# Two Fourier and gated layers on one core: separate homes for the last block's row tiles, a later difference step, a gap in the tests, and a new order of the opening

## The chip, the cores and the metric

The kernel runs on one core of a Trainium2 chip. The metric is device time in microseconds (us), the median of several runs. One more execution was taken with the hardware profiler; all views of the profile come from it.

## The reference

The input `x` is 2048 rows by 640 columns. Two layers follow each other, each of them a Fourier mixing step and a gated step, both with a residual:

```python
def _A_ref(x, dft_seq_re, dft_seq_im, dft_hid_re, dft_hid_im):
    a = jnp.einsum("bsd,ed->bse", x, dft_hid_re)
    b = jnp.einsum("bsd,ed->bse", x, dft_hid_im)
    return jnp.einsum("ts,bse->bte", dft_seq_re, a) - jnp.einsum("ts,bse->bte", dft_seq_im, b)

def _B_ref(x, w_gate, w_up, w_down):
    g = jnp.einsum("bsd,df->bsf", x, w_gate)
    u = jnp.einsum("bsd,df->bsf", x, w_up)
    return jnp.einsum("bsf,fd->bsd", _sigmoid(g) * u, w_down)

x = A_x
for _ in range(2):
    x = x + _A_ref(_layernorm(x), ...)
    x = x + _B_ref(_layernorm(x), ...)     # w_gate, w_up: 640 x 1728, w_down: 1728 x 640
```

## The kernel before

All matrix work is done in 16-bit floats, each operand as a high half and a low half, with three products for one. The Fourier matrices are used through their symmetries: rows and columns are folded onto each other, which cuts the products; the kernel tests on the way that the given matrices have these symmetries, and a general program stands behind it for the case that they haven't. Rows are taken in four blocks of 512 (`block`, `last` is the fourth). In the gated step of most blocks seven products of half size do the work of eight (`seven`, line 1516, by way of `products`, lines 1434 to 1448).

**The opening** (line 1780) is everything until layer 1's first gated products. SyncE's queue issues the loads in a fixed order: the rows of `x` in groups A to D for each of four parts, the Fourier matrices, the hidden ones, the first weights. Then a long table of names, `OPENING` (line 160), is read from left to right; each name calls one function, which emits its instructions. On every engine the instructions stand in that order, and an engine takes them strictly in turn. The names that matter here: `turn i g` lets TensorE reverse the rows of a group with a reversing matrix (line 404), `turned` copies the result back on ScalarE (line 410), `ident 0` makes the second reversing matrix (lines 357 and 358), `stats` takes a group's mean and variance (line 482), `cg` and `col` fold columns (lines 734 and 735), `row n` folds the one odd row, `chi` and `clo` make high and low halves of the Fourier matrix, `join` adds folded rows (line 869), `jhi` and `jlo` make their halves (lines 886 and 896), `seq` is the product along the sequence (line 1035), `ev` and `evhi` take its sums out of PSUM (lines 269 and 271), `nst`, `cen`, `nhi`, `nlo`, `tp`, `tph` and `tpl` are the norm ahead of the gated step: statistics, centring (line 518), high and low halves (lines 544 and 547), transposes on TensorE (line 669) and the copies that follow them (lines 677 and 679). `wshi` and `wslo` split a weight tile. `junk n` emits n small products whose result nobody reads (line 380); they fill TensorE's time while it has nothing else.

**After the opening** the work is a list of steps, one for each piece of TensorE's work. `at(u, f, ...)` puts a function before step `u`; what shares a step is sorted by the fraction of `u`, and `run` puts a list of functions in order at one place. In layer 2 the norm of the first rows stands at `he + 10`: `norm_turned(r, 0)` and `norm_turned(r, 1)` make the halves of row tile `r`, and `first_differences` (line 1192) makes two differences for a sum that is needed later (line 1197).

**Row tiles of a block.** While a block's products run, the next block's rows are prepared in two pairs of row tiles, `i` = 0 and 1. For each, `pair_apply` (line 603) writes the normed rows to a tile `pf`, `pair_combine` (lines 610 to 613) adds combinations, `pair_parts` (lines 621 and 622) writes the halves to a tile `pb`, and `pair_transpose` (line 626) issues two transposing transfers on SyncE's queue from `pb` to the operand that TensorE reads, and gives `pb` back.

**Homes.** Tiles share one large buffer. `take` asks for a number of units and `drop` gives them back; the kernel is first recorded without addresses, `find_homes` (line 99) then places all tiles so that two which are held at the same time do not overlap, the largest first, keeping tiles apart in time where it can, and the kernel is recorded again with these addresses. So a tile that is held longer can change the address of many others, and an instruction that writes to an address waits for the last reader of what was there before. The loads of the products' weights (`G`, `S` and `U` with the tile's number: lines 1362, 1364, 1366 and 1368, in SyncE's queue) are among these. `hv` is a tile of gate values, read last by line 1513.

**Tests.** The tests of the Fourier matrix load rows or columns by GpSimd's queue (lines 1663 and 1680) into a `room`, compare on VectorE (lines 1669 to 1689) and add up squares on ScalarE (line 1635). In layer 1, 42 of them are spread evenly from `block[1] + 6` to `block[3] + 13`: the load at `u`, the test 1.2 and the squares 1.95 spacings later. Two rooms are fixed; a third and further ones are taken from the large buffer when the two are in use.

Of the kernel before, what the change touches and what calls it, by code (L numbers as in the profile page):

```python
# [18 lines left out]
D = 640  # L19
# [119 lines left out]
class Slot:  # L139
# [18 lines left out]


OPENING = """  # L160
    turn 0 B, turned 0 B, stats 0 D, cg 0 3, stats 0 A, cg 0 1, ident 0, turn 0 C, junk 13, turned 0 C, means 0,
    turn 1 C, turn 1 B, chi 0 0, square 0 B, chi 1 0, double 0, square 0 C, turned 1 B, clo 1 0, turned 1 C, junk 13,
    ident 2, stats 1 A, cg 0 2, means 1, square 1 B, power 0, chi 1 1, col 1 0, junk 13, junk 8, scale 0, clo 0 0,
    stats 1 D, cg 0 0, col 1 1, turn 2 B, dg 0, square 1 C, mj 0, turned 2 B, power 1, stats 2 A, turn 2 C,
    turned 2 C, double 1, ps 0, junk 15, double 2, scale 1, junk 10, ro 1 1, chi 1 2, means 2, col 2 1, row 0,
    col 2 0, row 1, clo 1 1, junk 3, turn 3 B, whhi 1, re 1 0, ro 1 0, square 2 B, square 2 C, re 1 1, clo 1 2,
    chi 0 1, whlo 1, stats 2 D, whhi 2, jhi 0 o, junk 14, junk 5, de 1 0, de 1 1, do 1 1, do 1 0, join 1, junk 1,
    whhi 5, chi 0 2, jhi 1 o, power 2, junk 4, whhi 0, scale 2, row 2, turned 3 B, ro 2 0, re 2 0, jhi 0 e, jhi 1 e,
    re 2 1, whlo 5, jlo 0 o, whlo 0, jlo 1 o, clo 0 1, jlo 0 e, turn 3 C, junk 4, junk 5, turned 3 C, free, col 3 0,
    stats 3 A, junk 2, seq 0 1, whhi 3, ro 2 1, c512hi, jlo 1 e, row 3, dd 2 0, seq 1 1, stats 3 D, means 3, col 3 1,  # L170
    c512lo, seq 0 0, evhi 0 1 0, wshi 0 1, evhi 0 1 1, whlo 3, dd 2 1, chi 1 3, square 3 C, square 3 B, ev 0 1 0,
    junk 5, join 2, ev 0 1 1, clo 1 3, power 3, double 3, jhi 2 e, evhi 0 1 2, scale 3, chi 0 3, ro 3 1, seq 1 0,
    re 3 1, junk 14, jhi 2 o, re 3 0, junk 12, whhi 4, ro 3 0, evhi 0 0 0, clo 0 2, jlo 2 e, clo 0 3, ev 0 1 2,
    dd 3 1, junk 18, jlo 2 o, junk 14, dd 3 0, join 3, ident 1, whlo 4, ev 0 0 0, evhi 0 0 2, seq 2 1, jhi 3 e,
    jhi 3 o, wshi 2 0, evhi 0 0 1, wshi 1 1, jlo 3 e, jlo 3 o, seq 2 0, whlo 2, ev 0 0 1, wslo 1 1, ev 0 0 2, seq 3 0,
    seq 3 1, evhi 1 0 1, wshi 2 1, evhi 1 0 0, evhi 1 1 1, hid 0 0, evhi 1 0 2, ev 1 0 0, ev 1 0 1, ev 1 1 1,
    evhi 1 1 2, evhi 1 1 0, wslo 0 1, ev 1 0 2, first 1, first 0, wshi 1 0, hid 0 1, ev 1 1 0, wslo 1 0, im, sums,
    hid 1 0, hidev 1 0, hid 1 1, hid 2 0, add 0, nst 0, hidev 1 1, wshi 0 0, cen 0, difs, add 1, hidev 2 0, nst 1,
    nvar 0, ev 1 1 2, wslo 0 0, npow 0, nscale 0, nst 2, cen 1, nst 3, nhi 0, nhi 1, nvar 1, nlo 0, wld 4 0, wld 4 1,
    cen 3, mid, hid 2 1, nlo 1, npow 1, tp 0, tp 1, tph 0, wld 3 1, wld 3 0, tpl 0, tpl 1, nscale 1, tph 1, cen 2,  # L180
    wslo 2 0, nhi 3, nhi 2, midhi, gu 0 0, hidev 2 1, nlo 2, nlo 3, tp 2, tp 3, tpl 2, tph 3, hid 3 0, wshi 3 0,
    hidev 3 0, hid 3 1, tph 2, wshi 4 1, wshi 3 1, tpl 3, wshi 4 0, hidev 3 1, wslo 3 1, wslo 3 0, gu 1 0, gu 0 1,
    gu 1 1, wslo 2 1, wslo 4 1, middif, wslo 4 0, gu 2 0, gu 2 1"""

ON_ACT = {(2, GA), (2, GD), (3, GA), (3, GD)}
# [41 lines left out]
def folded(ctx, tc, pool, dram, big, acc, flag, homes, x, ct, wh, wg, wu, wc, wd, out):  # L227
# [19 lines left out]
    turn = [0]  # L247
# [46 lines left out]
    def at(u, f, *a):  # L294
        jobs[max(0, int(u // 1))].append((u, f, a))
# [158 lines left out]
    stats = {}  # L454
# [119 lines left out]
    def place(b):  # L574
        return (b + len(other)) % 2
# [47 lines left out]
        if n == 3:  # L623
            drop("pf", b, i)

    def pair_transpose(b, i):
        for q, src in enumerate(held["pb", b, i].parts):
            nc.sync.dma_start(XW[place(b)][:, :, q, i * P : (i + 1) * P], src, transpose=True)  # L628
        drop("pb", b, i)


    FT = XO["T1"]
# [1216 lines left out]
    last = NB - 1  # L1849
# [3 lines left out]
    for layer in range(2):  # L1853
        first = layer == 0
# [9 lines left out]
        block = []  # L1864
# [16 lines left out]
        def run(u, todo):  # L1881
            for n, (f, *a) in enumerate(todo):
                at(u + 0.001 * n, f, *a)

        def evictions(ph, tps=(EV, OD)):
            return [(evict_sums, ph, tp, d) for tp in tps for d in (1, 0, 2)]
# [40 lines left out]
        else:  # L1927
# [3 lines left out]
            odd = [[(f, *key, (n,)) for n in range(2)] for ph in range(2) for f, *key in evictions(ph, (OD,))]  # L1931
# [281 lines left out]
```

## Time and profile before

| | |
|---|---|
| time, median of 3 runs | 1136.33 us (1135.86 to 1137.09) |
| time of the profiled execution | 1136.34 us |
| its span, first to last instruction | 1134.5 us |
| granted TensorE clock | 0.999 |
| busy: PE, PEld, DVE, ACT, POOL | 1118.4, 892.3, 757.5, 539.5, 347.7 us |
| matmuls | 9123 |

PE is TensorE's products, PEld its loads of weights, DVE VectorE, ACT ScalarE, POOL GpSimd, SP SyncE; SPq is SyncE's queue. In the timeline a row gives start, duration, engine, line, operation, tiles and shapes, the count of merged instructions, and in brackets the engine's idle time before it with what ended it. In the view of waits a row gives who waited for whom, the total, the number of times and the longest. Busy time of TensorE counts products that overlap, so the distance from one start to the next tells more than the duration of one.

### The profile page before, as it was taken

The numbers are of one execution on the slowest core, as the hardware profiler recorded it, in microseconds if no ns is written. First come the engines' busy times: TensorE is split into PE (matmuls) and PEld (weight loads), VectorE is DVE, ScalarE is ACT, GpSimd is POOL, SyncE is SP. The second block draws the span as 40 slices with busy tenths as digits, with TensorE's granted clock in tenths as the row PEclk, the third lists the DMA queues.
The fourth block names the chain that finished last, engine by engine and source line by source line (L and its number), as shares of the span: only waits on it lengthen the run. The fifth ranks groups of instructions, "written<-read, shape, count | busy, mean of one in ns | idle before, by whom it ended". The sixth has DMA issues, their size and how long they took to land. (4 is left out here: it accounts for less than half of the span.)

```text
span 1134.5 us, 23654 instructions
## 1 busy us (share of the span) xinstructions
PE 1118.4 (99%) x9123; PEld 892.3 (79%) x9123; DVE 757.5 (67%) x1679; ACT 539.5 (48%) x1191; POOL 347.7 (31%) x568
## 2 busy tenths in 40 slices
PE   7999999999999999999999999999999999999998
PEld 5777446788878887888878888778877888778875
DVE  7984897866656776576668877834764578426751
ACT  7985583355524653265525545214642555225430
POOL 1001653332555452521440203032554222132001
PEclk9999999999999999999999999999999999999999
DMA  8533885777495767968522672575857973799511
GB/s 248 188 106 110 300 319 150 232 232 248 140 264 187 246 183 167 257 221 292 179 99 76 160 228 83 141 235 183 249 174 184 291 232 108 88 237 292 161 42 39
DMA packets 154448, 214.74 MB, mean 189 GB/s; under 512 B 74655, under 2 KB 99505, under 8 KB 154326
## 3 DMA queue, kind: packets, MB, share of 16 engines
q1 hardware_dynamic: 135622, 165.04, 49.5%
q0 software_dynamic: 18560, 47.93, 13.9%
q8 instruction: 73, 1.20, 0.4%
q14 instruction: 49, 0.40, 0.1%
q10 hardware_dynamic: 144, 0.16, 0.0%
HBM read 173.04 MB, written 25.44 MB: 175 GB/s over the span
## 5 line engine op out<-in xcount | busy, mean ns | idle before, releaser
L1445 PE MATMUL acc<-big 128*128 128x256 f16 x4698 | 516.5, 273 | 1.1 <-DMA big<-big 1.1
L1445 PEld LDWEIGHTS <-big 128*128 128x128 f16 x4698 | 459.7, 98 | 55.4 <-issue 1.3
L1602 PE MATMUL acc<-big 128*128 128x320 f16 x2624 | 357.7, 299 | 0.0
L1602 PEld LDWEIGHTS <-big 128*128 128x128 f16 x2624 | 256.8, 98 | 99.5
L1663 POOL DMA_DIRECT2D big<-in_ct x256 | 174.7, 688 | 263.6 <-DVE big L1672 136.0
L1449 ACT ACTIVATE big<-acc 128x256 f32<-128x256 f32 x348 | 130.8, 382 | 242.4 <-PE acc L1445 235.7
L1513 DVE TENSOR_TENSOR big<-big 128x512 f16<-128x512 f32 x87 | 60.0, 689 | 114.1 <-ACT big L1512 114.0
L1635 ACT ACTIVATE big<-big 128x768 f32<-128x768 f32 (+10 forms) x110 | 81.3, 739 | 82.4 <-DVE big L1672 64.2
L1398 PE MATMUL acc<-big 128*128 128x256 f16 (+1 forms) x705 | 114.6, 325 | 0.5 <-ACT big L677 0.5
L1398 PEld LDWEIGHTS <-big 128*128 128x128 f16 x705 | 68.9, 98 | 45.0 <-issue 0.7
L1491 ACT ACTIVATE big<-big 128x512 f32<-128x512 f32 x87 | 53.4, 627 | 50.2 <-DVE big L1482 49.6
L271 DVE SCALAR_TENSOR_TENSOR big<-big 128x640 f16<-128x640 f32 (+7 forms) x82 | 61.2, 778 | 11.8 <-ACT big L269 9.4
L1501 DVE SCALAR_TENSOR_TENSOR big<-acc,big 128x256 f32<-128x256 f32 x87 | 36.4, 419 | 41.4 <-PE acc L1445 35.9
L1617 DVE SCALAR_TENSOR_TENSOR big<-acc,big 128x320 f32<-128x320 f32 x64 | 28.3, 484 | 52.8 <-PE acc L1602 52.7
L621 ACT ACTIVATE big<-big 128x384 f16<-128x384 f32 (+2 forms) x48 | 28.6, 645 | 70.1 <-DVE big L603 48.6
L269 ACT ACTIVATE big<-big 128x640 f16<-128x640 f32 (+7 forms) x82 | 51.3, 657 | 20.8 <-POOL big L1336 6.6
L1482 DVE TENSOR_TENSOR big<-big,acc 128x512 f32<-128x512 f32 x87 | 59.2, 681 | 1.3 <-PE acc L1445 1.1
L1512 ACT ACTIVATE big<-big 128x512 f16<-128x512 f32 x87 | 54.4, 626 | 8.1 <-DVE big L1503 7.0
L1680 POOL DMA_DIRECT2D big<-in_ct x40 | 27.4, 689 | 92.3 <-ACT big L1635 58.3
L442 POOL DMA_INDIRECT out<-big,rows x8 | 9.3, 1165 | 123.3 <-DVE fin L1760 55.1
L1481 DVE TENSOR_TENSOR big<-big 128x256 f32<-128x256 f32 x87 | 36.4, 418 | 7.7 <-ACT big L1449 7.6
L1669 DVE TENSOR_TENSOR big<-big 128x256 f32<-128x256 f32 x64 | 26.5, 415 | 21.5 <-DMA big<-in_ct 21.5
(252 smaller groups left out, 1100.4 us busy)
## 6 DMA issues: line engine op xcount, KB each, us to landing
big<-kept_s SPq DMA_DIRECT2D x84, 512.0 KB, 6.8
big<-kept_w SPq DMA_DIRECT2D x115, 320.0 KB, 5.0
big<-in_ct POOLq DMA_DIRECT2D x256, 128.0 KB, 4.8
big<-kept_w SPq DMA_DIRECT2D x74, 192.0 KB, 5.8
kept_w<-big SPq DMA_DIRECT2D x27, 320.0 KB, 3.4
big<-in_ct POOLq DMA_DIRECT2D x32, 256.0 KB, 5.3
kept_s<-big SPq DMA_DIRECT2D x13, 512.0 KB, 7.1
big<-in_wg SPq DMA_DIRECT2D x18, 320.0 KB, 4.9
```

Source lines behind the costliest of these rows:

```text
L269: nc.scalar.activation(dh, src, AF.Copy, scale=s)
L271: nc.vector.scalar_tensor_tensor(dl, src, s, dh, op0=OP.mult, op1=OP.subtract)
L1398: nc.tensor.matmul(ps, w[wp][:, d * P : (d + 1) * P], xt[:, xp, :], start=(d == 0 and wp == HI and xp == HI), stop=(d == ND - 1 and wp == LO))
L1445: nc.tensor.matmul(ps, wt, xt, start=start and n == 0, stop=n == len(todo) - 1, skip_group_check=not start)
L1449: nc.scalar.activation(dst, ps, AF.Copy)
L1482: nc.vector.tensor_tensor(v, v, other, op=OP.add)
L1491: nc.scalar.activation(v, v, AF.Sigmoid, scale=SG)
L1512: nc.scalar.activation(s.parts[HI], v, AF.Copy)
L1513: nc.vector.tensor_tensor(s.parts[LO], v, s.parts[HI], op=OP.subtract)
L1602: nc.tensor.matmul(held["pd", e][0][:, :EH], held["ht", j].parts[hp][:, i * P : (i + 1) * P], held["w", 2, j].parts[wp][:, e * EH : (e + 1 ...
L1635: nc.scalar.activation(v, v, AF.Square, accum_out=new_sum()[:p])
L1663: nc.gpsimd.dma_start(v[:, g], bass.AP(ct.tensor, (r * S + row) * S, [[P, NS], [d * S, 16], [1, P]]))
```

## The change

Four things are changed.

1. `pair_transpose` gets an argument `apart`. In layer 2's last block `pb` of the first pair is no longer given back after its transposes, but together with that of the second pair. So the tiles of the two pairs are held at the same time and get addresses of their own.
2. At `he + 10` the two differences stand behind the low halves instead of ahead of them.
3. The 42 tests of layer 1 are drawn together so that a gap of two steps opens from 1.5 steps ahead of `block[last]` on; the distance from a load to its test and its squares stays. A test's squares now come after the load of the second test behind it, so a third room is in use in turn.
4. The table `OPENING` is in another order at four places, and has 162 junk products for 173.

```diff
-    def pair_transpose(b, i):
+    def pair_transpose(b, i, apart=False):
         for q, src in enumerate(held["pb", b, i].parts):
             nc.sync.dma_start(XW[place(b)][:, :, q, i * P : (i + 1) * P], src, transpose=True)
-        drop("pb", b, i)
+        for k in (() if apart and not i else (0, 1) if apart else (i,)):
+            drop("pb", b, k)
...
             run(he + 10, [(norm_centre, 0), (norm_centre, 1), (norm_step, 0), (norm_turned, 0, 0),
-                          odd[4][1], (first_differences, (0,)), (norm_turned, 0, 1), (norm_turned, 1, 0), (norm_turned, 1, 1)])
+                          odd[4][1], (norm_turned, 0, 1), (norm_turned, 1, 0), (norm_turned, 1, 1), (first_differences, (0,))])
...
-                at(u + 1.1, pair_transpose, b, i)
+                at(u + 1.1, pair_transpose, b, i, not first and b == last)
...
+        def spaced(u, u0, u1):
+
+            gap = 1.5 + 0.5
+            u = u0 + (u - u0) * (u1 - u0 - gap) / (u1 - u0)
+            return u + gap if u > block[last] - 1.5 else u
+
         for u0, u1, n in free:
             pace = (u1 - u0) / n
             tight = first or u0 < block[1]
             for u in [u0 + pace * k for k in range(n)]:
+                if first and u0 < block[last]:
+                    u = spaced(u, u0, u1)
```

The first lines of the table, before and after:

```diff
-    turn 0 B, turned 0 B, stats 0 D, cg 0 3, stats 0 A, cg 0 1, ident 0, turn 0 C, junk 13, turned 0 C, means 0,
+    turn 0 B, turned 0 B, stats 0 D, cg 0 3, cg 0 1, ident 0, stats 0 A, turn 0 C, junk 13, turned 0 C, means 0,
```

Further on in it, `clo 1 0` goes behind `cg 0 2`; `col 2 1` goes from ahead of `row 0` to behind `clo 1 2`; `re 2 0` and `ro 2 0` change places; junk is thinned in three stretches (1 fewer ahead of `turn 2 B`, 7 fewer from there to `seq 0 1`, 3 fewer from there to `seq 2 1`); `wshi 0 0` goes ahead of `nst 0`, and `cen 3` from ahead of `mid` to behind `tph 1`.

VectorE at the start of the opening. Before, the statistics of group A (lines 482 and 483) and a fold stand ahead of the reversing matrix (lines 357 and 358):

```order
L483 BN_AGGR quad_73<-quad_73 128x2
L734 TENSOR_TENSOR big<-big 128x320
L735 TENSOR_TENSOR big<-big 128x320
L482 BN_STATS quad_73<-big 128x6 x2
L483 BN_AGGR quad_73<-quad_73 128x2
L734 TENSOR_TENSOR big<-big 128x320
L735 TENSOR_TENSOR big<-big 128x320
L357 TENSOR_SCALAR big<-big 128x128
L358 MEMSET big 1x1
L271 SCALAR_TENSOR_TENSOR big<-big 128x514
```

Now (line numbers below line 626 are one higher):

```order
L483 BN_AGGR quad_73<-quad_73 128x2
L735 TENSOR_TENSOR big<-big 128x320
L736 TENSOR_TENSOR big<-big 128x320
L735 TENSOR_TENSOR big<-big 128x320
L736 TENSOR_TENSOR big<-big 128x320
L357 TENSOR_SCALAR big<-big 128x128
L358 MEMSET big 1x1
L482 BN_STATS quad_73<-big 128x6 x2
L483 BN_AGGR quad_73<-quad_73 128x2
L360 TENSOR_SCALAR big<-big 128x128
```

The reversing matrix has come ahead of the statistics, and the low half of the Fourier matrix (line 271, `clo 1 0`) has gone further back.

VectorE at the norm of layer 2, before: an eviction (line 271), the two differences (line 1197), the low halves of the first two row tiles (line 547), an eviction, the copies after the transposes (line 679).

```order
L271 SCALAR_TENSOR_TENSOR big<-acc_490,big 128x512
L1197 TENSOR_TENSOR big<-big 128x322 x2
L547 SCALAR_TENSOR_TENSOR big<-big,small_78 128x640 x2
L271 SCALAR_TENSOR_TENSOR big<-acc_64,big 128x512
L679 COPY big<-acc_485 128x5x128
L679 COPY big<-acc_487 128x5x128
```

Now:

```order
L271 SCALAR_TENSOR_TENSOR big<-acc_484,big 128x512
L547 SCALAR_TENSOR_TENSOR big<-big,small_78 128x640 x2
L1198 TENSOR_TENSOR big<-big 128x322 x2
L271 SCALAR_TENSOR_TENSOR big<-acc_64,big 128x512
L680 COPY big<-acc_479 128x5x128
L680 COPY big<-acc_481 128x5x128
```

Only the differences and the low halves have changed places.

ScalarE at the norm at the opening's end, before: centring (line 518), a root (427), statistics (492, 493), high halves (544), the centring `cen 3`, a root, the copies after the transposes (677), `cen 2`.

```order
L518 ACTIVATE big<-big,small_78 128x640
L492 ACTIVATE big,small_79<-big 128x640
L493 ACTIVATE big,small_79<-big,small_79 128x640
L544 ACTIVATE big<-big,small_78 128x640 x2
L518 ACTIVATE big<-big,small_79 128x640
L427 ACTIVATE small_79<-small_79 128x2
L677 ACTIVATE big<-acc_486 128x5x128
L677 ACTIVATE big<-acc_485 128x5x128
L518 ACTIVATE big<-big,small_79 128x640
L544 ACTIVATE big<-big,small_79 128x640 x2
L1169 ACTIVATE big<-acc_489 128x321
```

Now:

```order
L518 ACTIVATE big<-big,small_78 128x640
L492 ACTIVATE big,small_79<-big 128x640
L493 ACTIVATE big,small_79<-big,small_79 128x640
L544 ACTIVATE big<-big,small_78 128x640 x2
L427 ACTIVATE small_79<-small_79 128x2
L678 ACTIVATE big<-acc_480 128x5x128
L678 ACTIVATE big<-acc_479 128x5x128
L518 ACTIVATE big<-big,small_79 128x640 x2
L544 ACTIVATE big<-big,small_79 128x640 x2
L1170 ACTIVATE big<-acc_483 128x321
```

`cen 3` has gone behind the copies, which follow the high halves and one root now.

The homes move no instruction; on SyncE the order is the same as before. What changes there are the addresses, and with them which earlier reader a load or a write waits for.

More of the change, by code (lines that the diff above doesn't have):

```diff
@@ L160 @@
 OPENING = """
-    turn 0 B, turned 0 B, stats 0 D, cg 0 3, stats 0 A, cg 0 1, ident 0, turn 0 C, junk 13, turned 0 C, means 0,
-    turn 1 C, turn 1 B, chi 0 0, square 0 B, chi 1 0, double 0, square 0 C, turned 1 B, clo 1 0, turned 1 C, junk 13,
-    ident 2, stats 1 A, cg 0 2, means 1, square 1 B, power 0, chi 1 1, col 1 0, junk 13, junk 8, scale 0, clo 0 0,
+    turn 0 B, turned 0 B, stats 0 D, cg 0 3, cg 0 1, ident 0, stats 0 A, turn 0 C, junk 13, turned 0 C, means 0,
+    turn 1 C, turn 1 B, chi 0 0, square 0 B, chi 1 0, double 0, square 0 C, turned 1 B, ident 2, turned 1 C, junk 13,
@@ L164 @@
+    stats 1 A, cg 0 2, clo 1 0, means 1, square 1 B, power 0, chi 1 1, col 1 0, junk 14, junk 6, scale 0, clo 0 0,
     stats 1 D, cg 0 0, col 1 1, turn 2 B, dg 0, square 1 C, mj 0, turned 2 B, power 1, stats 2 A, turn 2 C,
-    turned 2 C, double 1, ps 0, junk 15, double 2, scale 1, junk 10, ro 1 1, chi 1 2, means 2, col 2 1, row 0,
-    col 2 0, row 1, clo 1 1, junk 3, turn 3 B, whhi 1, re 1 0, ro 1 0, square 2 B, square 2 C, re 1 1, clo 1 2,
-    chi 0 1, whlo 1, stats 2 D, whhi 2, jhi 0 o, junk 14, junk 5, de 1 0, de 1 1, do 1 1, do 1 0, join 1, junk 1,
@@ L168 @@
[L168 to L182, printed above, removed]
+    turned 2 C, double 1, ps 0, junk 15, double 2, scale 1, junk 10, ro 1 1, chi 1 2, means 2, row 0, col 2 0, row 1,
@@ new lines @@
+    clo 1 1, junk 3, turn 3 B, whhi 1, re 1 0, ro 1 0, square 2 B, square 2 C, re 1 1, clo 1 2, col 2 1, chi 0 1,
+    whlo 1, stats 2 D, whhi 2, jhi 0 o, junk 15, junk 2, de 1 0, de 1 1, do 1 1, do 1 0, join 1, junk 1, whhi 5,
+    chi 0 2, jhi 1 o, power 2, junk 4, whhi 0, scale 2, row 2, turned 3 B, re 2 0, ro 2 0, jhi 0 e, jhi 1 e, re 2 1,
+    whlo 5, jlo 0 o, whlo 0, jlo 1 o, clo 0 1, jlo 0 e, turn 3 C, junk 4, turned 3 C, junk 2, free, col 3 0,
+    stats 3 A, seq 0 1, whhi 3, ro 2 1, c512hi, jlo 1 e, row 3, dd 2 0, seq 1 1, stats 3 D, means 3, col 3 1, c512lo,
@@ L183 @@
+    wslo 2 0, nhi 2, nhi 3, midhi, gu 0 0, hidev 2 1, nlo 2, nlo 3, tp 2, tp 3, tpl 2, tph 3, hid 3 0, wshi 3 0,
+    hidev 3 0, hid 3 1, tph 2, wshi 4 1, wshi 3 1, tpl 3, wslo 3 1, wslo 3 0, gu 1 0, wshi 4 0, hidev 3 1, gu 0 1,
     gu 1 1, wslo 2 1, wslo 4 1, middif, wslo 4 0, gu 2 0, gu 2 1"""
```

10 lines of the change are left out of this document (added).

## The prediction

> **What bounds the kernel now.** I read the busy time by stage first, since a mean over the span hides where an engine waits. Columns: stretch (us), its length, busy time of PE, PEld, DVE, ACT and POOL with counts, granted clock, DMA share, GB/s.
>
> ```profile
> 0.00:82.16 82.16, 73.70 (x515) 55.48 (x516) 70.00 (x166) 68.15 (x160) 7.62 (x47) 1.00 0.57 180
> 82.16:619.50 537.34, 537.33 (x4311) 418.79 (x4310) 376.33 (x828) 264.06 (x560) 217.03 (x330) 1.00 0.67 205
> 619.50:633.70 14.20, 13.30 (x143) 11.27 (x141) 10.62 (x22) 10.43 (x23) 5.71 (x10) 1.00 0.52 169
> 633.70:1003.00 369.30, 369.30 (x3102) 303.18 (x3100) 236.22 (x530) 151.66 (x332) 101.33 (x165) 1.00 0.66 183
> 1003.00:1004.40 1.40, 0.30 (x4) 0.10 (x2) 0.89 (x2) 0.00 (x0) 0.00 (x0) 1.00 0.72 157
> 1004.40:1134.50 130.10, 124.51 (x1059) 103.51 (x1058) 63.45 (x134) 45.14 (x119) 15.99 (x17) 0.99 0.52 150
> ```
>
> From 82.16 to 619.50 and from 633.70 to 1003.00 PE is busy without a gap, so TensorE is the bound there and nothing that the change does to VectorE, ScalarE or the queues in those stretches can gain anything; it can only cost, by opening a gap. Time is to be had in three places: the opening (PE idle 8.46 of 82.16), the norm of layer 2 (0.90 of 14.20) and the start of layer 2's last block (1.10 of 1.40). The tail's idle time lies after the last matmuls and isn't touched. Who ends those waits, from the view of waits (total, times, longest):
>
> ```profile
> PE acc L1445 <- DMA big<-big: 1.1, 1, 1.1
> PE acc L669 <- DVE big L547: 1.1, 2, 0.6
> PE twin L404 <- DVE big L358: 1.0, 1, 1.0
> ```
>
> These three are just what three of the edits aim at: transposes that land late, the low halves of the norm, and the matrix that turns rows around. So each edit is worth at most its row, and the question is what is late next.
>
> **Homes apart.** The timeline around the last block, PE, then SyncE's queue, then VectorE:
>
> ```profile
> 1003.03 0.27 PE L1445 MATMUL acc<-big 128*128 128x256 f16 x1
> 1004.39 5.84 PE L1445 MATMUL acc<-big 128*128 128x256 f16 x52 [1.10 <-DMA big<-big]
> 970.22 12.68 SPq L628 DMA_TRANSPOSE big<-big  x2
> 992.68 0.35 SPq L447 DMA_DIRECT2D out<-big  x1
> 993.13 7.65 SPq L628 DMA_TRANSPOSE big<-big  x2
> 972.32 0.41 DVE L1689 TENSOR_TENSOR big<-big 1x256 f32<-1x256 f32 x1
> 986.45 1.14 DVE L603 TENSOR_SCALAR big<-big,small 128x640 f32<-128x640 f32 x2 [13.72 <-DMA big<-big]
> 991.77 1.68 DVE L1617 SCALAR_TENSOR_TENSOR big<-acc,big 128x320 f32<-128x320 f32 x4
> ```
>
> VectorE finished a test at 972.73 and then stood until 986.45: the second pair of row tiles shares its home with the first pair's parts, which the first two transposes still read. Its own two transposes were issued from 993.13 to 1000.78, and PE's second matmul of the block came 1.36 after the first, where 52 matmuls in 5.84 put them 0.11 apart: 1.25 lost. With the homes apart, VectorE starts the second pair at 972.7 and is through it in 991.77 - 986.45 = 5.3, at 978.0. The same engine's evictions (L1617) follow 13.7 earlier, and so does the store L447 that stands between the two pairs of transposes on SyncE's queue. What is late next is that queue itself: the first pair holds it to 982.90. The second pair then takes 7.65 to 12.68 (its own row, and the row of the first, which ran beside test loads), and lands some 3.6 after its last issue (1000.78 to PE's 1004.39): by 994.5 to 999.6. PE asks at 1003.03, so 3.4 to 8.5 us of cover are left. Gain: **1.25**; 0 only if the second pair should take over 16 us.
>
> **Later differences.** Around the norm of layer 2, VectorE, ScalarE, PE:
>
> ```profile
> 617.98 0.68 DVE L271 SCALAR_TENSOR_TENSOR big<-acc,big 128x512 f16<-128x512 f32 x1
> 618.58 0.89 DVE L1197 TENSOR_TENSOR big<-big 128x322 f32<-128x322 f32 x2
> 619.38 1.67 DVE L547 SCALAR_TENSOR_TENSOR big<-big,small 128x640 f16<-128x640 f32 x2
> 621.57 0.88 DVE L679 COPY big<-acc 128x640 f16<-128x640 f16 x2
> 618.14 1.55 ACT L544 ACTIVATE big<-big,small 128x640 f16<-128x640 f32 x2
> 620.32 1.25 PE L669 MATMUL acc<-ident,big 128*128 128x128 f16 x15 [0.60 <-DVE big L547]
> 624.02 3.44 PE L1398 MATMUL acc<-big 128*128 128x256 f16 x30
> ```
>
> The two differences (L1197) take VectorE from 618.58 to 619.38, and the low halves (L547) wait behind them. Put behind, they free 0.80, but a low half needs its high half (L544), ready at 618.14 + 1.55/2 = 618.92 at the earliest. So L547 moves from 619.38 to 618.92 at best: 0.46. I take **0.4** for the hand-over between the engines. VectorE stands from 618.58 to 618.92 for it, and all that follows on it is 0.34 later, the copies L679 too: 622.45 becomes 622.8, while PE wants them at 624.02 - 0.4 = 623.6. That holds. Bounds: 0.46, and 0.3 if the second half of the norm, which hangs on the same VectorE queue, gives a tenth back.
>
> **The opening.** Phase one moves `ident 0` (L357, L358) ahead of `stats 0 A` (L482 and one short instruction, about 1.0 of VectorE). VectorE's rows, PE's, SyncE's and the issue's time to landing:
>
> ```profile
> 9.39 0.88 DVE L482 BATCH_NORM_STATS2 quad<-big 128x6 f32<-128x320 f32 x2
> 11.52 0.06 DVE L358 MEMSET big<- 1x1 f32 x1
> 11.71 2.39 PE L404 MATMUL twin<-big 128*128 128x320 f32 x8 [1.03 <-DVE big L358]
> 7.58 0.32 SPq L399 DMA_DIRECT2D big<-in_x  x1
> big<-in_x SPq DMA_DIRECT2D x1, 37.5 KB, 4.4
> ```
>
> The profile names L358, done at 11.58. But the same matmuls read the rows whose last piece SyncE issued at 7.58; the smaller piece before it took 4.4 to land, and at that rate this one is there at 11.98. PE began at 11.71, so it took less, yet by the nearest row it lands within tenths of L358. With the identity 1.0 earlier PE still waits for the load: I take 0.05, between 0 and 1.0. The other phases:
>
> ```profile
> 24.11 0.83 DVE L734 TENSOR_TENSOR big<-big 128x640 f32<-128x640 f32 x1 [0.55 <-ACT big L748]
> 25.64 0.66 ACT L809 ACTIVATE big<-big,quad 1x321 f32<-1x321 f32 x1
> 31.56 1.56 DVE L869 TENSOR_TENSOR big<-big 128x641 f32<-128x641 f32 x2
> 34.01 0.72 ACT L886 ACTIVATE big<-big 128x640 f16<-128x640 f32 x1
> 34.96 0.17 DVE L434 SCALAR_TENSOR_TENSOR quad<-quad 128x4 f32<-128x4 f32 x1 [1.84 <-ACT quad L429]
> 49.01 6.50 PE L380 MATMUL acc<-big 128*128 128x256 f16 x58
> 59.07 5.03 PE L1035 MATMUL acc<-big 128*128 128x256 f16 x42 [0.28 <-DVE big L271]
> 81.04 1.12 DVE L679 COPY big<-acc 128x640 f16<-128x640 f16 x2
> 80.85 1.27 ACT L677 ACTIVATE big<-acc 128x640 f16<-128x640 f16 x2
> ```
>
> `col 2 1` (1.6 of VectorE) goes behind `clo 1 2`. VectorE then does `col 2 0` to 25.7, waits for ScalarE's row (26.30) and loses 0.6, so the join L869 ends at 33.7 for 33.1; ScalarE's L886 wants it at 34.01, and the 1.84 before L434 takes up the rest: 0. Junk falls from 173 to 162 matmuls, 11 times 6.50/58 = 0.11: 1.2 of PE time, but it is filler ahead of waits. Around the stretch at 49.01 three fewer only let PE reach its wait for L271 (59.07) 0.3 sooner: 0. Phase four lets ScalarE's copies (L677, ended 82.12) go one activation earlier, before `cen 3`; VectorE's copies (L679) still end at 82.16, so PE gains at most one matmul: 0.1. Together the opening gives **0.1**, bounds 0 and 1.1 (the identity's whole 1.0, were the load no hindrance).
>
> On filler the Trainium skill (TensorE: Matmul & The Clock Gate, "HAM oscillation — how this bites in real kernels") speaks against the change: an idle stretch of about 3.4 us returns the array to half clock. Here the granted clock is 1.00 in all of 0 to 82.16, and by the terms above no pause grows by more than 0.6 (five matmuls fewer ahead of `seq 0 1`).
>
> **Pause of tests.** The tests of layer 1 move in time, some by a few us, inside 82.16 to 619.50 where PE has no gap: no gain is possible. They also take a third room in turn, so the homes of many tiles change, and a load may wait for a tile that is released later. The longest such hold that matters is in the last block:
>
> ```profile
> 1028.56 0.32 SPq L1362 DMA_DIRECT2D big<-kept_w  x1
> 1037.01 0.69 DVE L1513 TENSOR_TENSOR big<-big 128x512 f16<-128x512 f32 x1 [0.76 <-ACT big L1512]
> ```
>
> The load of `G 8` (L1362) now lies where `hv 3` lay, whose last reader is that L1513: issue at 1037.7 for 1028.56. Four pairs of tiles run ahead of its own, 45 matmuls each for the first two tiles and 54 for the six after: 414 at 0.109 from 1004.39 is 1049.5. About 5 us of landing (the x load's 4.4, rounded up) put the tile at 1042.7. Cost 0, with 6.8 us of cover.
>
> **Sum.** 1.25 + 0.4 + 0.1 = 1.75 off the profiled execution: span 1134.5 to 1132.75, its time 1136.34 to 1134.6; the median of the runs, 1136.33, is the same number. Forecast **1134.6**. 0.2% is 2.27 us, about what a measurement of this kernel can tell from no change: the forecast lies inside it.
>
> **Rivals.**
> - The opening does move: L358, as the profile names it, was the last to be waited for, and ScalarE's dense chain carries the 1.0 on. For: the named row. Against: the load's issue time. 1.25 + 0.4 + 1.1 = 2.75: 1133.6. Chance 0.22.
> - The transposes stay late, because the second pair collides with loads that also come forward. For: the first pair's 12.68 against 7.65. Against: 3.4 us of cover. Then 0.5 is left: 1135.8. Chance 0.07.
> - A held load becomes the bound: `G 8`, and behind it in SyncE's queue the rest of its group. It decides from an issue later than 1049.5 - 5 = 1044.5. Were the tile before it in that home released a pair later, at 1049.5, the load would land at 1054.5 and PE lose 5.0: 5.0 - 1.75 gives 1139.6, slower than before. Against: the cover. Chance 0.04.
> - The clock falls in a thinned pause: the 42 matmuls at 59.07 at half clock take 10.06 for 5.03, 1139.6. That is the rule of the Trainium skill above; the granted 1.00 speaks against it. Chance 0.02.
>
> **Numbers.** The forecast keeps 0.65; its own range is 1133.9 to 1135.3 (gain 1.0 to 2.4, from the bounds of the terms and the 0.8 by which the runs of before, 1135.86 to 1137.09, differ from their median). The range reaches to the first two rivals: 1133.2 to 1136.0. Faster by over 0.2% means below 1134.06: the first rival and a tenth of the forecast, 0.22 + 0.07 = 0.29. Slower: the last two, 0.06. Within: 0.65.
>
> **What would show it.** Right: PE's second matmul of the last block 0.11 after the first; the second pair of transposes issued from about 983; L547 at about 618.9 less the opening's gain, its wait on PE near 0.2; L404 still at about 11.7 with L358 done near 10.5. Wrong: L404 near 10.7 (first rival); a wait of PE on L1362, L1364 or L1366 loads, or a gap in a stretch that has none now; a granted clock under 0.99 before 82.

## The result, and the profile after

The changed kernel takes 1134.91 us (median of 22 runs, 1134.41 to 1137.11), the kernel before 1136.40 in the same runs (22, 1135.01 to 1141.77): ratio 0.9987, 95% interval 0.9981 to 0.9993. Forecast was 1134.6, with a range of 1133.2 to 1136.0. The profiled execution took 1135.11, its span is 1133.3 (before 1136.34 and 1134.5).

The busy time by stage after; columns as in the prediction, the stretches moved by what the kernel gained up to there:

```profile
0.00:82.04 82.04, 72.39 (x505) 54.38 (x506) 69.84 (x165) 67.60 (x159) 7.08 (x47) 1.00 0.57 179
82.04:619.30 537.26, 537.22 (x4308) 418.52 (x4307) 375.82 (x826) 264.91 (x561) 216.63 (x330) 1.00 0.68 205
619.30:633.30 14.00, 13.24 (x142) 11.43 (x140) 11.35 (x24) 10.50 (x23) 4.71 (x8) 1.00 0.53 167
633.30:1002.00 368.70, 368.70 (x3098) 302.80 (x3098) 236.28 (x531) 151.57 (x332) 102.42 (x168) 1.00 0.69 185
1002.00:1003.00 1.00, 1.00 (x9) 0.68 (x7) 0.10 (x1) 0.00 (x0) 1.00 (x1) 1.00 1.09 223
1003.00:1133.30 130.30, 124.58 (x1060) 103.53 (x1058) 64.27 (x136) 45.30 (x119) 14.95 (x17) 0.99 0.48 147
```

The stretch at the start of layer 2's last block, 1.10 idle of 1.40 before, is full in this view. The two long stretches are full as they were, and the granted clock is the same. The norm of layer 2 is idle for 0.76 where it was 0.90.

The last block in the timeline: TensorE, VectorE, SyncE's queue. Line numbers below line 626 are one higher than before.

```profile
1002.83 7.38 PE L1446 MATMUL acc<-big 128*128 128x256 f16 x65
972.49 1.12 DVE L603 TENSOR_SCALAR big<-big,small 128x640 f32<-128x640 f32 x2
970.04 12.39 SPq L628 DMA_TRANSPOSE big<-big  x2
982.53 1.49 SPq L447 DMA_DIRECT2D out<-big  x1
984.12 13.74 SPq L628 DMA_TRANSPOSE big<-big  x2
997.92 0.59 SPq L1363 DMA_DIRECT2D big<-kept_w  x1
1036.38 0.32 SPq L1363 DMA_DIRECT2D big<-kept_w  x1
```

VectorE starts the second pair at 972.49 with no wait (986.45 before, after 13.72 of waiting). Its transposes are issued 9 us sooner, and the weight loads behind the transposes start at 997.92 for 1000.87. But the second pair takes longer: 13.74 to issue for 7.65, and by the trace's completions (the times at which the DMA engines report a transfer done) the last transpose lands at 1003.0, 5.1 after the last issue, where it was 3.6. So of the 9 us 1.3 are left at the landing, and that is just too late. The row at 1002.83 merges 65 products. In a narrower window it has four:

```profile
1002.83 0.72 PE L1446 MATMUL acc<-big 128*128 128x256 f16 x4
```

Four products 0.11 apart, the last 0.27 long, take 0.60. The other 0.12 lies ahead of the second product, which needs these transposes and starts at 1003.06, 0.23 after the first. So 0.12 of the 1.25 is still lost. The row at 1036.38 is the held load of `G 8`, with nothing waiting for it.

The norm of layer 2. First two rows of TensorE before, then VectorE, ScalarE and TensorE after.

```profile
619.27 0.44 PE L669 MATMUL acc<-ident,big 128*128 128x128 f16 x5
621.50 2.69 PE L1120 MATMUL acc<-big 128*1 128x322 f16 x26
```

```profile
611.12 0.89 DVE L1189 SCALAR_TENSOR_TENSOR big<-acc,big 128x322 f32<-128x322 f32 x2 [0.33 <-ACT big L269]
619.18 1.68 DVE L547 SCALAR_TENSOR_TENSOR big<-big,small 128x640 f16<-128x640 f32 x2 [0.35 <-ACT big L544]
619.77 2.06 ACT L1170 ACTIVATE big<-acc 128x322 f32<-128x322 f32 x6
619.21 0.44 PE L670 MATMUL acc<-ident,big 128*128 128x128 f16 x5
620.24 1.13 PE L670 MATMUL acc<-ident,big 128*128 128x128 f16 x15 [0.58 <-ACT big L1170]
621.30 2.69 PE L1121 MATMUL acc<-big 128*1 128x322 f16 x26
```

L547 now waits for its high half (L544), as it should. But it starts at 619.18, not 618.9, and the transposes at 620.24 no longer name it: they name L1170, ScalarE's copies that empty a PSUM bank. From the high halves' transposes to the products behind (619.21 to 621.30) it is 2.09, before 2.23 (619.27 to 621.50).

The opening. First TensorE's first gated product before, then VectorE and TensorE after.

```profile
82.17 2.02 PE L1398 MATMUL acc<-big 128*128 128x256 f16 x17 [0.54 <-ACT big L677]
```

```profile
10.18 0.06 DVE L358 MEMSET big<- 1x1 f32 x1
11.76 0.51 PE L404 MATMUL twin<-big 128*128 128x320 f32 x1 [1.64 <-DMA big<-in_x]
81.92 3.30 PE L1399 MATMUL acc<-big 128*128 128x256 f16 x27 [0.28 <-ACT big L678]
```

The matrix is done at 10.24 for 11.58, and L404 starts at 11.76 for 11.71, now with the load as the named wait.

### The profile page after: what moved, and what is told of

The parts are those of the page before. It is cut to its first block, busy times and chain, and to the rows that moved or that the text cites. A ratio compares the mean times of both kernels' runs of the same rounds, so it can differ in the third digit from the quotient of the medians.

```text
span 1133.3 us, 23690 instructions
## 1 busy us (share of the span) xinstructions
PE 1117.1 (99%) x9112; PEld 891.3 (79%) x9112; DVE 757.7 (67%) x1679; ACT 539.9 (48%) x1191; POOL 346.8 (31%) x568
## 5 line engine op out<-in xcount | busy, mean ns | idle before, releaser
L271 DVE SCALAR_TENSOR_TENSOR big<-big 128x640 f16<-128x640 f32 (+7 forms) x82 | 61.4, 779 | 11.1 <-ACT big L269 8.8
L269 ACT ACTIVATE big<-big 128x640 f16<-128x640 f32 (+7 forms) x82 | 51.3, 658 | 21.0 <-POOL big L1337 6.6
L1482 DVE TENSOR_TENSOR big<-big 128x256 f32<-128x256 f32 x87 | 36.3, 417 | 8.8 <-ACT big L1450 8.7
L622 DVE TENSOR_TENSOR big<-big 128x384 f16<-128x384 f32 (+2 forms) x48 | 34.2, 750 | 7.1 <-DMA big<-big 7.0
```

The source lines that it names most:

```text
L269: nc.scalar.activation(dh, src, AF.Copy, scale=s)
L271: nc.vector.scalar_tensor_tensor(dl, src, s, dh, op0=OP.mult, op1=OP.subtract)
```

## Experiments

### The four parts, each alone on the kernel before

Each is that part of the change's diff and nothing else. In these runs the kernel before took 1136.24 (29 runs).

**Homes apart alone.**

```diff
-                at(u + 1.1, pair_transpose, b, i)
+                at(u + 1.1, pair_transpose, b, i, not first and b == last)
```

> The kernel before with the homes apart alone: in layer 2's last block the parts of both pairs of row tiles keep their places until the second pair is transposed; opening, differences and tests stand as before. By the prediction's term: the gap of TensorE at 1003 goes and the time falls by 1.25 (ratio 0.9989), with the opening and the norm at the same times as before. Rival (the gain of the last block needs tiles that the pause of tests moved, or the transposes collide with loads): VectorE starts the second pair at 972.7, but TensorE still waits at 1003, and less than 0.5 is gained. A third reading, that the moved homes cost something elsewhere, would show as a new wait of TensorE between 82 and 1003.

Measured: 1135.52 (11 runs, 1134.79 to 1137.61), ratio 0.9992 (0.9983 to 1.0001). VectorE's L358, TensorE's L404 and its last block:

```profile
10.94 0.06 DVE L358 MEMSET big<- 1x1 f32 x1
11.68 0.51 PE L404 MATMUL twin<-big 128*128 128x320 f32 x1 [2.18 <-DMA big<-in_x]
1002.88 7.37 PE L1446 MATMUL acc<-big 128*128 128x256 f16 x66
```

The gap at the last block is gone. The median moved by 0.72 and not by 1.25, and the interval just reaches no change; the kernel before doesn't lose 1.25 there each time (below). A by-product: in the old order the matrix was done at 11.0 in this execution, and L404 still started at 11.68, when the load landed.

**Later differences alone.**

```diff
-  odd[4][1], (first_differences, (0,)), (norm_turned, 0, 1), (norm_turned, 1, 0), (norm_turned, 1, 1)])
+  odd[4][1], (norm_turned, 0, 1), (norm_turned, 1, 0), (norm_turned, 1, 1), (first_differences, (0,))])
```

> The kernel before with the differences (L1197) behind the low halves (L547) alone. Forecast term: 0.4 off, first transpose of a low half at 619.9 for 620.32. Theory now (the next wait is the PSUM bank that ScalarE's evictions, L1169, free from 619.6 on, and in the changed kernel the chain ahead was 0.3 late as well): L547 at 618.95, the transposes of the low halves at 620.05 to 620.1 with ScalarE's L1169 named as what they waited for, 0.2 to 0.25 off in time. If the chain ahead is late here too (VectorE's L1188 at 611.1 for 610.83), the lateness hangs on the order of these instructions and not on the other parts, and 0.15 is gained.

Measured: 1135.74 (11 runs, 1135.25 to 1137.42), ratio 0.9996 (0.9986 to 1.0005), so the times alone show no change; the profile does. TensorE in the norm, in an execution in which all of it lay 1.9 later, 1.7 of it for waits for ScalarE (L1449) in layer 1:

```profile
621.22 0.44 PE L669 MATMUL acc<-ident,big 128*128 128x128 f16 x5
622.00 1.13 PE L669 MATMUL acc<-ident,big 128*128 128x128 f16 x15 [0.35 <-ACT big L1169]
623.07 1.65 PE L1120 MATMUL acc<-big 128*1 128x322 f16 x14
```

From 621.22 to 623.07 it is 1.85, 0.38 less than before: the forecast's 0.4, with the bank named and not L547. VectorE's L1188 did not wait here. So the bank is the next limit, but it isn't what made the gain small in the changed kernel: that was the wait of 0.33 at L1189. It stands in five of the eight profiles that have opening, differences and pause together, and in none of the other six. Among the kernels with the later differences the stretch takes 2.09 or 2.10 where the wait stands and 1.85 or 1.86 where not (the kernel that reorders it left aside). In the five, the first L1189 starts 0.23 after the last of ScalarE's copies out of PSUM ahead of it (L269) has ended; in the other nine it starts 0.12 or 0.13 before that copy ends, so it doesn't wait for it there. A moved home isn't the reason: by the kernels' own placement (`find_homes`) all tiles of the changed kernel, which waits, lie where they lie in the kernel with the loads ahead (below), which doesn't. The traces don't keep the values that a semaphore is waited for, and the cause stays open.

**The opening alone.**

```diff
-OPENING = """  (the table before)
+OPENING = """  (the table after)
```

> The kernel before with the new order of the opening alone. Theory (the load of x for the second tile holds the turn at 11.7, not the matrix L358): L404's second group stays at 11.6 to 11.8 with a wait on the load named, L358 done at about 10.3; the first gated matmul at 82.17 comes 0.05 to 0.25 earlier; ratio 0.9998 to 1.0. Rival of the prediction (the matrix was the last to be waited for): L404 at 10.7 and the gated matmuls 1.0 earlier, ratio 0.9991. The rest of the kernel moves as a whole.

Measured: 1138.60 (7 runs, 1137.08 to 1140.58), ratio 1.0026 (1.0014 to 1.0037), slower, which neither theory had. By the kernel's placement the homes of all tiles are as before. The profile is of the fastest of these runs; TensorE:

```profile
82.03 1.23 PE L1398 MATMUL acc<-big 128*128 128x256 f16 x8 [0.28 <-ACT big L677]
1003.74 10.53 PE L1445 MATMUL acc<-big 128*128 128x256 f16 x95 [0.40 <-DMA big<-big]
1015.44 14.80 PE L1445 MATMUL acc<-big 128*128 128x256 f16 x134 [1.17 <-DMA big<-kept_w]
```

The opening itself is hardly slower: the first gated product is at 82.03 for 82.17, TensorE's products at 607 (L1120) at 607.32 for 607.26. What this execution lost more than the kernel before, it lost in layer 2's last block, to a weight load (kept_w) that the kernel before did not wait for; the transposes cost it 0.56, less than the 1.25 before. Its longer runs have no profile.

**The pause alone.**

```diff
+                if first and u0 < block[last]:
+                    u = spaced(u, u0, u1)
```

> The kernel before with the pause of tests alone (the tests of layer 1 squeezed together so that two steps' worth around the last block have none). Theory: no change (ratio 0.9997 to 1.0003): TensorE has no gap between 82 and 619.5 before or after. Rival (moved homes make a load or a write wait): a new wait of TensorE or of VectorE's chain at 603 to 620, with VectorE's L1188 at 611.1 for 610.83 and the transposes at 620.32 up to 0.3 later; 0.1 to 0.3 lost.

Measured: 1136.37 (11 runs, 1135.59 to 1138.03), ratio 1.0004 (0.9995 to 1.0013): no change, as forecast. VectorE's L1188 was on time. This execution too waits for a weight load (kept_w) in the last block, 0.33 at 1026.40, and loses less to the transposes, 0.48. The medians of the four parts sum to 1.27 slower; together they are 1.49 faster.

### What the homes apart are worth with the rest

**The changed kernel without them**: the differences, the opening and the pause on the kernel before. In these runs the kernel before took 1136.89 (32 runs).

```diff
-        for k in (() if apart and not i else (0, 1) if apart else (i,)):
-            drop("pb", b, k)
+        drop("pb", b, i)
```

> The changed kernel without the homes apart (opening, differences and pause only). The parts alone do not add up: homes apart 0.7 faster, differences 0.5 faster, opening 2.4 slower, pause 0.1 slower in the medians, sum 1.3 slower, and the whole is 1.5 faster. Theory: what the opening alone lost lies in layer 2's last block, where transposes and the weight loads behind them on SyncE's queue come within tenths of being late, so that a small shift of everything before decides which are; then this kernel loses there too: 1136.5 to 1138.5, with waits of TensorE on loads of kept_w or on the transposes between 1003 and 1030. Rival (the opening costs by itself): the loss shows between 0 and 82 or before 1003. Third: the order alone was an accident of those runs and this kernel takes 1136.0 (before less the differences and the opening).

Measured: 1141.07 (9 runs, 1135.62 to 1142.90), ratio 1.0026 (1.0010 to 1.0042). TensorE, and SyncE's second pair of transposes:

```profile
1003.32 0.27 PE L1445 MATMUL acc<-big 128*128 128x256 f16 x1
1008.56 21.69 PE L1445 MATMUL acc<-big 128*128 128x256 f16 x185 [4.97 <-DMA big<-big]
993.08 8.56 SPq L628 DMA_TRANSPOSE big<-big  x2
```

The second pair is issued when it was before (993.13, 7.65 long), yet the gap is 5.24 for 1.36. The view of the DMA issues in the 20 us up to 1003 gives the median time from a transpose's issue to its landing; first the kernel before, then the changed kernel, then this one:

```profile
big<-big SPq DMA_TRANSPOSE x2, 6.1
```

```profile
big<-big SPq DMA_TRANSPOSE x2, 8.3
```

```profile
big<-big SPq DMA_TRANSPOSE x2, 10.8
```

The theory holds, though the loss is larger than the 1136.5 to 1138.5 that was expected: it lies where the homes apart act, and it is no fixed sum. Moved addresses aren't its cause: by the kernels' placement this kernel has the homes of the pause alone, which loses nothing, and the opening alone, which loses, has those of the kernel before. The first two products of the block lie 1.36 (kernel before), then 0.76, 0.67, 0.59 and 5.24 apart in the five profiles above without separate homes, where 0.11 is no gap.

**Opening and homes apart together**, neither differences nor pause:

```diff
+OPENING = """  (the table after)
+                at(u + 1.1, pair_transpose, b, i, not first and b == last)
```

> The kernel before with the opening and the homes apart, and neither the differences nor the pause. Theory (the homes apart bring transposes and weight loads 3 us forward and so take the loss away that the opening alone showed): 1134.9 to 1135.4, no wait of TensorE between 633 and 1003 and none on kept_w after it. Rival (the opening costs 2.4 by itself): 1137.9. If the two only add up with their medians: 1136.24 - 0.72 + 2.36 = 1137.9 as well.

Measured: 1135.46 (11 runs, 1134.55 to 1136.15), ratio 0.9988 (0.9980 to 0.9997). TensorE in the last block, 654 products in one piece:

```profile
1004.02 71.56 PE L1446 MATMUL acc<-big 128*128 128x256 f16 x654
```

No wait for kept_w is left. By the medians the homes apart take 0.72 off the kernel before, 3.14 off the kernel with the new opening, 6.16 off the kernel with all other parts. By the ratios to the kernel before in the same runs it is 0.9, 4.3 and 4.4, so the last two aren't told apart.

**Fewer tests, without the homes apart.** Three tests of wh, the Fourier matrices along the hidden side, are left out of the kernel that took 1141.07; here the kernel before took 1136.20 (35 runs).

```diff
+                if load is load_hidden_rows and key[0] == 0 and key[1] > 0:
+                    continue
                 at(block[2] + u, load, *key)
```

> The changed kernel without the homes apart, as run before at 1141.1, with three of the tests of wh left out (rows 1 to 3 of the first half: loads L1723 on GpSimd's queue, VectorE's L1727 and ScalarE's squares). In that kernel's trace the last low half of the second pair landed between 1005.2 and 1008.5, while loads of these tests and the first weight loads shared the DMA engines. Theory (the loads of the tests between 990 and 1008 draw the landing out): the gap after the first matmul of the last block falls under 1, the time to 1135.2 to 1136.2, and the runs lie within 1.5 of each other. Rival (the weight loads right behind the transposes on SyncE's queue, or the stores, draw it out): the times stay spread, 1137 to 1142.

Measured: 1135.09 (12 runs, 1134.54 to 1135.79), ratio 0.9986 (0.9976 to 0.9997). TensorE and SyncE's second pair:

```profile
1002.74 7.48 PE L1445 MATMUL acc<-big 128*128 128x256 f16 x67
992.43 7.38 SPq L628 DMA_TRANSPOSE big<-big  x2
```

The transposes are issued at much the same time and nothing waits for them. In the kernel with the tests GpSimd's queue issued the loads of two tests beside them, four transfers of 200 KB from 990.32 to 1002.22; here the next such load is issued at 1000.86. The completions in the trace say it too: here the last transpose lands at 1001.4 to 1001.6 on all its DMA engines, in the kernel with the tests between 1005.2 and 1008.5. So other traffic draws the landing out, in good part that of GpSimd's queue; the left-out tests also took work from VectorE and ScalarE and changed which rooms are used, and weight loads and stores were not tried. The Trainium skill (DMA: Bandwidth & Descriptors, "Queues, rings and completion order") says that each DMA engine takes turns between the queues that have work for it; the later landings here are in keeping with that, but no view shows the turns themselves. Why the kernel before met the collision less often than the two that are slower isn't shown.

### The opening's loads

**The clearing ahead.** On the changed kernel:

```diff
+        nc.gpsimd.memset(take(5, "cx").f32[:, : SB + 2], 0.0)
         start_masks()
...
-        v = take(5, "cx").f32[:, : SB + 2]
-        nc.gpsimd.memset(v, 0.0)
+        v = held["cx"].f32[:, : SB + 2]
```

> The changed kernel with one clearing (L982, GpSimd) ahead of the row lists (L280 iota). In the trace GpSimd starts its first iota 9.6 us after the instruction before it with no wait that the profile shows, the clearing stands behind the iotas and ends at 14.3, and SyncE's queue stands from 11.96 to 14.30 for it, with the loads of the third tile behind. Theory: SyncE's queue goes on at 12.0, the third group of turns L404 starts at 16.5 to 17.5 instead of 18.35, and 0 to 0.3 is gained at the first gated matmul (81.9), since ScalarE and VectorE have no more idle time than that before 24. Rival (the eight transfers in flight are the limit, not the clearing): SyncE's next issue moves by under 0.5 and nothing follows.

Measured: 1135.32 (11 runs, 1133.84 to 1137.25) against 1136.89, ratio 0.9988 (0.9979 to 0.9997): as the changed kernel. GpSimd and SyncE's queue in the changed kernel, then SyncE's queue in this one:

```profile
13.00 0.37 POOL L280 IOTA rows<- 128x1 int32 x4 [9.56 <-issue]
13.76 0.52 POOL L982 MEMSET big<- 128x514 f32 x1
14.30 0.82 SPq L984 DMA_DIRECT2D big<-in_ct  x3
```

```profile
13.10 0.81 SPq L983 DMA_DIRECT2D big<-in_ct  x3
```

SyncE's queue went on 1.2 sooner, not 2.3: in place of 1.6 for the clearing it now waits there 0.8 for a load of x in flight. The third group of turns came at 17.78 for 18.35, and nothing of it reached the end.

**The loads ahead as well.** With it, the loads of x for the second tile's turned groups stand ahead of the first two pieces of ct, and ScalarE's splits of these behind the squares:

```diff
+        for g in (GB, GC):
+            load_x(1, g)
         for r in range(2):
             load_c(r, 0)
...
-    turn 1 C, turn 1 B, chi 0 0, square 0 B, chi 1 0, double 0, square 0 C, turned 1 B,
+    turn 1 C, turn 1 B, square 0 B, square 0 C, double 0, chi 0 0, chi 1 0, turned 1 B,
```

> The changed kernel with the clearing ahead as in the kernel beside it and also with the loads of x for the second tile (its two turned groups) ahead of the first two pieces of ct, whose splits L269 go behind the squares L419 on ScalarE. Theory (the load holds the second group of turns, not the matrix L358): L404's second group starts at 10.3 to 10.7 for 11.76, now held by the matrix or by the filler before it; ScalarE's dense chain and the first gated matmul move by up to 1.4, of which I expect 0.5 to 1.0 to reach 81.9 (ratio to before 0.9980 to 0.9984). Rival of the prediction (the matrix held it and the load was hidden): L404 stays at 11.7 and the time at the changed kernel's. A third: the pieces of ct then come too late for ScalarE and VectorE and it is 0.5 slower.

Measured: 1134.43 (11 runs, 1133.75 to 1134.95), ratio 0.9978 (0.9970 to 0.9987). TensorE:

```profile
10.95 2.42 PE L404 MATMUL twin<-big 128*128 128x320 f32 x8 [0.17 <-DVE big L358]
81.52 1.67 PE L1398 MATMUL acc<-big 128*128 128x256 f16 x12 [0.28 <-ACT big L678]
```

The turns moved by 0.8, and now it is the matrix that they wait for: in the changed kernel it was the load. Of the 0.8, 0.4 reached the first gated product, where 0.5 to 1.0 was expected.

**The matrix late again**, with the loads ahead:

```diff
-    cg 0 3, cg 0 1, ident 0, stats 0 A, turn 0 C,
+    cg 0 3, stats 0 A, cg 0 1, ident 0, turn 0 C,
```

> The kernel with both edits of the opening's loads, with the matrix (ident 0) back behind stats 0 A, where it stood before the change. Theory (the load held the second group of turns in both of the compared kernels; with the load ahead the matrix is the next to hold it): L404's second group at 11.6 to 11.9, with VectorE's L358 named and done just before, for 10.95 with the matrix early; 0.2 to 0.6 slower than that kernel (1134.4). Rival (only the load matters): 10.95 stays.

Measured: 1134.47 (12 runs, 1133.94 to 1135.85), ratio 0.9981 (0.9968 to 0.9994):

```profile
11.30 1.07 PE L404 MATMUL twin<-big 128*128 128x320 f32 x3 [0.85 <-DVE big L358]
81.46 1.77 PE L1398 MATMUL acc<-big 128*128 128x256 f16 x13 [0.28 <-ACT big L678]
```

The wait went to the matrix as expected, but the turns started at 11.30 and not at 11.6 or later, and the 0.2 to 0.6 that it was expected to cost did not come. So the matrix's new place is worth nothing measurable, with the load late (L404 at 11.71 before and 11.76 after) or early. The loads' place is worth 0.5 by the medians (1134.43 for the changed kernel's 1134.91), and all 11 runs lie at or under 1134.95, though the two ratios' intervals overlap (0.9970 to 0.9987, 0.9981 to 0.9993).

**A square ahead of the scaled matrices**, on ScalarE, with the loads ahead:

```diff
-    turn 2 B, dg 0, square 1 C, mj 0,
+    turn 2 B, square 1 C, dg 0, mj 0,
```

> The kernel with both edits of the opening's loads, and on ScalarE the square of the second tile's group C (L419) ahead of the scaled matrices (L836), which wait there 0.5 for VectorE. Theory (ScalarE's chain from 14 to 56 is dense, so a filled gap moves what follows): the first gated matmul 0.2 to 0.5 earlier than 81.52, the time 1133.9 to 1134.2. Rival (the scaled matrices and the products on TensorE that hang on them are what VectorE's chain waits for, 0.9 later now): no gain, or 0.4 slower.

Measured: 1134.28 (12 runs, 1133.13 to 1135.03), ratio 0.9976 (0.9964 to 0.9988), first gated product at 81.22: 0.3 sooner in the profile, not to be told from 1134.43 in the times. These kernels are the fastest of the study.

### The bank in the norm

With the loads ahead, ScalarE's copies of `hidden 1 1` stand ahead of the second high half:

```diff
-  odd[4][1], (norm_turned, 0, 1), (norm_turned, 1, 0), (norm_turned, 1, 1), (first_differences, (0,))])
-            run(he + 11, [(evict_hidden, 1, 1), (evict_hidden, 2, 0)])
+  odd[4][1], (norm_turned, 0, 1), (evict_hidden, 1, 1), (norm_turned, 1, 0), (norm_turned, 1, 1), (first_differences, (0,))])
+            run(he + 11, [(evict_hidden, 2, 0)])
```

> The kernel with both edits of the opening's loads, and in layer 2's norm ScalarE's two evictions of hidden 1 1 (the first of L1169) moved ahead of the second high half (L544). Theory (PE's first low-half transposes wait for the PSUM bank that these evictions free, 0.1 after the low half itself is there): the first group of low-half transposes then starts 0.94 after L547 starts, as in the kernel before, with L547 named, 0.1 sooner than with L1169 named; but the second low half is 0.7 later for its high half, so the matmuls after them win nothing: 0 to 0.5 slower. Rival (another wait stands behind the one named): the transposes of the first low half do not move.

Measured: 1135.09 (12 runs, 1134.38 to 1136.25), ratio 0.9988 (0.9978 to 0.9999). VectorE and TensorE:

```profile
618.20 0.88 DVE L547 SCALAR_TENSOR_TENSOR big<-big,small 128x640 f16<-128x640 f32 x1 [0.35 <-ACT big L544]
619.14 0.90 PE L670 MATMUL acc<-ident,big 128*128 128x128 f16 x10 [0.47 <-DVE big L547]
620.51 0.45 PE L670 MATMUL acc<-ident,big 128*128 128x128 f16 x5 [0.47 <-DVE big L547]
```

The first low half's transposes follow L547 by 0.94 (620.32 - 619.38 = 0.94 before, 620.24 - 619.18 = 1.06 in the changed kernel) and name it again: the bank was the limit, by 0.12. The second low half pays for it: from 618.23 to the products at 620.89 it is 2.66, for 1.85 with the loads ahead alone, and by the medians 0.66 is lost against 1134.43.

## Why the prediction was right, and where not

- **Homes apart, 1.25.** Between the two profiled executions it is 1.13: the gap of 1.36 became 0.23, where 0.11 is no gap. The steps held (VectorE from 972.5, queue held to 982.5, second pair from 984), but the cover was mis-sized: 13.74 to issue where 12.68 was the bound, and 5.1 to land where 3.6 was taken, so nothing was left of the 3.4 to 8.5 us and 0.12 was lost. The other profiles with separate homes land between 999.7 and 1002.9, 1.2 to 2.8 ahead of TensorE: the rival of transposes that stay late was nearer than its chance said. As a typical gain 1.25 is a draw. The step that failed is that one execution's gap was taken as the loss: it swings from 0.5 to 5.1, and what is gained depends on the other parts.
- **Later differences, 0.4.** The mechanism was right, and the size too where VectorE was on time (0.38). In the changed kernel's profile it is 0.14, for a late L1189 that no term had. The limit that came next, the bank, was not named; its price is 0.12.
- **Opening, 0.1.** Phase one: L404 waited for the load, as argued. Up to 59.07, phases one to three gave 0, and the wait for L271 grew by 0.33 (0.28 to 0.61) as the fewer fillers implied. Phase four brought the first gated product 0.25 forward, but the second starts 0.31 after it, at 82.22 for 82.28 (the 27 products of the row at 81.92 take 3.30, where 0.11 apart gives 3.1): it waits for VectorE's copy L680, which ends at 82.17 as it did before (82.16). So one product went ahead and 0.06 stays, just as the prediction argued from these copies. The table differs in two more places than were named (`nhi 2` and `nhi 3` change places, `wshi 4 0` and `hidev 3 1` go behind `gu 1 0`); from there to TensorE's products at 607 (L1121, before L1120) the two kernels take the same 524.98, so they cost nothing.
- **Pause, 0.** Right; the load of `G 8` was issued at 1036.38 where 1037.7 was worked out, less the 1.3 by which all was earlier.
- **The sum.** 0.06 + 0.14 + 1.13 = 1.33 against 1.75, for the span's 1.2. The medians agree better (1.49). That is in part luck: all three terms came out smaller in the profile, and the runs of the kernel before swing more than those of the changed one. That these swings make up the difference is argued, not shown. The range was wide as well: its upper end, 1136.0, is 0.33 from the time before.
- **The rivals.** The opening's 1.0 was refuted twice: in the old order the turns started at 11.68 with the matrix done at 11.0, and with the load ahead they moved. Transposes that stay late: with the homes apart none in seven of eight profiles, and 0.12 in the changed kernel's own. No held load in the changed kernel; without the homes apart a weight load behind the late transposes did hold TensorE in two profiles (1.17 and 0.33). The clock: 1.00 as before; the rule of the Trainium skill on idle stretches (TensorE: Matmul & The Clock Gate) found none long enough here: after the first products the longest is the 1.64 ahead of L404. That an edit of 0.1 in the opening could cost 2.4 without the homes apart was on no list: the terms were added as if they were independent.

## What to carry to other kernels

Where transfers of several queues meet just ahead of their use, as here, the gap in one profile is a draw, and terms need not add: look at the spread of the runs, and count an edit that brings such transfers forward by the spread that it ends. A part that is slower alone can be harmless in the whole, and the other way round. When a wait is taken away, ask for the next one by operand, output (the PSUM bank) and load, before sizing the gain.

## What was not expected of the hardware

- A pair of transposing transfers of the same size landed 1.8 (three tests fewer), 3.6 (kernel before) and 6.9 (changed kernel without separate homes) after its last issue, all issued from 992.4 to 993.1; brought forward to 984 it took 18.9 from first issue to landing, for 11.2 before.
- GpSimd's first iota started 9.56 after the instruction before it, with nothing that it waited for in the profile, and 10.70 in the kernel with the clearing ahead. The Trainium skill (GPSIMD Engine Reference, "2.1 Instruction dispatch") gives about 6 us without a visible instruction for the first call of freshly loaded code; whether it is that, no run here shows.
